# Giving the state matmuls of an attention kernel PSUM banks of their own, and packing three kinds of small matmuls into common runs

## The chip, the cores and the metric

The kernel runs on one core of a Trainium2 chip. The metric is the time of one execution on the device in microseconds (us), as a median over several executions; lower is better. The "span" in a profile is the same execution from its first to its last instruction, some 1.8 us shorter than the time.

## The reference

A block-wise linear attention with a decaying state feeds a feed-forward layer with a sine in it:

```python
for b in range(nb):                       # blocks of 64 positions, 12 of them
    intra = einsum('bhic,bhjc->bhij', qb, kb) * Dmask      # scores, masked
    intra = einsum('bhij,bhjd->bhid', intra, vb)
    inter = einsum('bhid,bhde->bhie', qb * lam_pow, kv_state)
    out[:, :, sl] = intra + inter
    kv_state = lam_block * kv_state + einsum('bhsd,bhse->bhde', kb * rev_pow, vb)
...
h = x @ w_in                              # x: 3072 tokens of 512 = the attention output
s = sin(alpha * h)
g = h + s * s / (alpha + 1e-09)
out = g @ w_out
```

## The kernel before

Tokens go through in six groups of 512. Each group has four attention *units* (24 in all), then 16 first-layer feed-forward blocks and 16 second-layer blocks of four 128x128 by 128x512 matmuls each. The order of all work on all engines is written out by hand in one list. An item names what is done, for which unit or block, on which engine (T TensorE, A ScalarE, V VectorE, G GpSimd, S SyncE, which issues the loads), and for PSUM users in which bank. Each engine follows its own items in that order.

Three item kinds use 64x64 quarters of the array: `s` (scores, 16 matmuls), `k` (state matmuls, 8 or 16) and `o` (masked scores times values, 16). The other TensorE items use the whole array: `oi` (query times state), `f1`, `f1a` and `f2` (feed-forward; `f1a` is half a block), `tq` and `tk` (transposes), `w` (warm-up matmuls on zeros), `lt` (the two halves of the last output tile); a single small `ap` belongs to the start. I call neighbouring `s`, `k` and `o` items with no whole-array item between them a *run*.

The parts that the change touches:

```python
BANK = ("h0", "h1", "h2", "h3", "s0", "s1")       # + "okv", one tile over two banks
HOLD = (0, 14)            # loads of group 1 wait for this first-layer block
...
def kvmm(u, bank, **_):                           # item k
    if u < 8:
        kps[u] = [psum([P, P], FP32, "kvp", i)[:] for i in bank]
    else:                                         # spare columns of the output pair
        okv[u] = ps.tile([P, 2, 512], FP32, name="okv", tag="okv", bufs=1)
        kps[u] = [okv[u][:, c, 2 * P:3 * P] for c in range(2)]
    ...
def interm(u, **_):                               # item oi
    okv[u] = ps.tile([P, 2, 512], FP32, name="okv", tag="okv", bufs=1)
    ...
def outev(u, c, eng, **_):                        # item x: output pair to SBUF
    cs = slice(c, c + 1) if u in XSPLIT else slice(0, 2)      # XSPLIT = (1, 2, 3)
    copy(eng, xt[g][:, 2 * hh:2 * hh + 2, bb, cs, :]..., okv[u][:, cs, 0:2 * P]...)
```

`kc` copies a state out of PSUM, `a` adds and decays it, `m` masks scores, `sin`, `sqr` and `stt` are the sine, its square and the sum of the feed-forward part, `ld` loads q, k or v of a unit, `tdq` and `tdk` transpose it by DMA, `wi` and `wo` load weights.

Of the kernel before, what the change touches and what calls it, by code (L numbers as in the profile page):

```python
# [18 lines left out]
tab:V ld.0.0:S sq.0:V ld.0.1:S sk.0:G w.4:T:h2 tq.0:T:2 tk.0:T:5 ld.0.2:S cv.0:A ld.1.0:S ld.1.1:S  # L19
k.0:T:0,1 a.0.0:V sk.1:V ld.1.2:S tcq.0:A tck.0:A w.4:T:s0 s.0:T kc.0.0:A sq.1:G oi.0:T tq.1:T:0  # L20
tcq.1:A tk.1:T:2 tck.1:A ld.2.0:S ld.2.1:S m.0.0:V m.0.1:V kc.0.1:V sq.2:V cv.1:A o.0:T x.0.0:A
sk.2:V s.1:T tq.2:T:0 tcq.2:A tk.2:T:2 tck.2:A w.3:T:h1 k.1:T:1,0 kc.1.0:A ld.2.2:S ld.3.0:S
ld.3.1:S ld.3.2:S wi.0:G wi.1:G sq.3:G cv.2:G cv.3:G n.0.0:G wi.2:G wi.3:G wo.0:G kc.1.1:A m.1.0:V
m.1.1:V a.1.0:V sk.3:V s.2:T wo.1:G a.0.1:G n.0.1:G m.2.0:V m.2.1:V oi.1:T tq.3:T:1 tcq.3:A tk.3:T:2
k.2:T:0,3 o.1:T x.1.0:V a.2.0:V tck.3:A w.3:T:s0 s.3:T kc.2.0:A kc.2.1:A x.1.1:A w.3:T:okv oi.2:T
o.2:T x.2.0:A m.3.0:V m.3.1:V x.2.1:A k.3:T:1,2 kc.3.0:A kc.3.1:A a.3.0:V ap:T al:V f1a.0.0:T:0
f1a.0.1:T:3 oi.3:T o.3:T f1a.0.2:T:4 f1a.0.3:T:5 x.3.0:V x.3.1:A f1.0.0:T f1.0.1:T sin.0.0:A
sin.0.1:A sqr.0.0:V sqr.0.1:G n.2.0:G wo.2:G f1.0.2:T f1.0.3:T sin.0.2:A stt.0.0:V sin.0.3:A
sqr.0.2:A sqr.0.3:A stt.0.1:V stt.0.2:V stt.0.3:V f1.0.4:T:2 sin.0.4:A sqr.0.4:V a.2.1:G n.2.1:G
f1.0.5:T:1 f1.0.6:T:0 sin.0.5:A sin.0.6:A sqr.0.5:V sqr.0.6:G stt.0.4:V stt.0.5:V stt.0.6:V  # L30
f1.0.7:T:3 f1.0.8:T:5 f1.0.9:T:4 sin.0.7:A sqr.0.7:A sin.0.8:A sin.0.9:A sqr.0.8:G sqr.0.9:G wo.3:G
n.3.0:G a.3.1:G stt.0.7:V stt.0.8:V f1.0.10:T:2 w.2:T:h0 f1.0.11:T:0 n.1.0:G stt.0.9:V sin.0.10:A
sqr.0.10:A stt.0.10:V a.1.1:G f2.0.0.0:T:3 sin.0.11:A sqr.0.11:V f1.0.12:T:5 f1.0.13:T:4 sin.0.12:A
sqr.0.12:A sin.0.13:A stt.0.11:V f1.0.14:T:2 sin.0.14:A sqr.0.13:A stt.0.12:V f2.0.0.1:T
f2.0.1.0:T:1 f1.0.15:T:0 sin.0.15:A f2.0.1.1:T f2.0.1.2:T sqr.0.14:G sqr.0.15:G f2.0.0.2:T
stt.0.13:V stt.0.14:V stt.0.15:V f2.0.2.0:T:2 f2.0.0.3:T oc.0.0:A f2.0.2.1:T f2.0.1.3:T ld.4.0:S
ld.4.1:S ld.4.2:S sq.4:G sk.4:G cv.4:A tq.4:T:3 tk.4:T:5 tcq.4:V tck.4:V oc.0.1:V ld.5.0:S ld.5.1:S
f2.0.2.2:T s.4:T m.4.0:V k.4:T:0,3 f2.0.2.3:T a.4.0:V m.4.1:V ld.5.2:S ld.6.0:S kc.4.0:A kc.4.1:A
cv.5:A ld.6.1:S ld.6.2:S ld.7.0:S ld.7.1:S ld.7.2:S oc.0.2:A sq.5:G sk.5:G tq.5:T:4 tk.5:T:1 oi.4:T
sq.6:G k.5:T:0,3 o.4:T sk.6:G cv.6:G sq.7:G tcq.5:A tck.5:V kc.5.0:A kc.5.1:V a.5.0:V n.5.0:G sk.7:G  # L40
s.5:T m.5.0:V x.4.0:A ld.8.0:S tq.6:T:2 tk.6:T:1 tck.6:A ld.8.1:S ld.8.2:S ld.9.0:S ld.9.1:S
f2.0.3.0:T:3 tcq.6:A m.5.1:V oi.5:T k.6:T:0,1 o.5:T a.6.0:V s.6:T kc.6.0:A ld.9.2:S ld.10.0:S
ld.10.1:S ld.10.2:S kc.6.1:A x.5.0:A tq.7:T:2 tcq.7:A f2.0.3.1:T tk.7:T:0 m.6.0:V m.6.1:V tck.7:V
oi.6:T f1a.1.0:T:1 o.6:T cv.7:G k.7:T:2,0 kc.7.0:A cv.8:A x.6.0:A n.1.1:G a.7.0:V s.7:T m.7.0:V
f2.0.3.2:T f2.0.3.3:T m.7.1:V oi.7:T o.7:T n.6.0:G n.4.0:G kc.7.1:V f1a.1.1:T:5 f1a.1.2:T:0 a.6.1:G
sq.8:G f1a.1.3:T:2 sk.8:G sq.9:G oc.0.3:A x.7.0:A f1.1.0:T f1.1.1:T f1.1.2:T f1.1.3:T f1.1.4:T:3
sin.1.0:A sin.1.1:A sqr.1.0:V sqr.1.1:V sk.9:G stt.1.0:V sin.1.2:A sqr.1.2:G sin.1.3:A sin.1.4:A
f1.1.5:T:4 f1.1.6:T:1 stt.1.1:V sqr.1.3:A stt.1.2:V sin.1.5:A stt.1.3:V sq.10:G k.8:T sqr.1.4:G
sin.1.6:A sqr.1.5:A sqr.1.6:A f1.1.7:T:0 kc.8:V ld.11.0:S f1.1.8:T:5 stt.1.4:V stt.1.5:V stt.1.6:V
sin.1.7:A cv.9:G k.9:T sin.1.8:A kc.9:V sk.10:G sqr.1.7:A sqr.1.8:A stt.1.7:V stt.1.8:V cv.10:G  # L50
sq.11:G n.3.1:G tdq.8:S tdq.9:S tdk.8:S f1.1.9:T:2 f1.1.10:T:3 f1.1.11:T:1 k.10:T sin.1.9:A
ld.11.1:S sk.11:G sqr.1.9:A ld.11.2:S tdk.9:S ld.12.0:S kc.10:A sin.1.10:A s.8:T sqr.1.10:A
f1.1.12:T:0 m.8.0:V a.8.0:G a.9.0:G m.8.1:V oi.8:T sq.12:G tdq.10:S tdk.10:S ld.12.1:S a.4.1:G s.9:T
o.8:T tdq.11:S tdk.11:S ld.12.2:S stt.1.9:V ld.13.0:S st.0.2.0:S f1.1.13:T:2 sin.1.11:A cv.11:A
stt.1.10:V sqr.1.11:A a.10.0:G x.8.0:A m.9.0:V m.9.1:V f2.1.0.0:T:3 n.10.0:G stt.1.11:V n.8.0:G
a.8.1:G ld.13.1:S st.0.1.0:S st.0.0.0:S st.0.0.1:S ld.13.2:S ld.14.0:S ld.14.1:S oi.9:T ld.14.2:S
tdq.12:S sin.1.12:A o.9:T x.9.0:V sin.1.13:A s.10:T m.10.0:V f2.1.0.1:T k.11:T f1.1.14:T:1 m.10.1:V
kc.11:V s.11:T oi.10:T a.11.0:G st.0.2.1:S m.11.0:V m.11.1:V ld.15.0:S ld.15.1:S ld.15.2:S ld.16.0:S
ld.16.1:S cv.12:A o.10:T x.10.0:A sqr.1.12:A f2.1.0.2:T sqr.1.13:G sin.1.14:A oi.11:T stt.1.12:V
o.11:T x.11.0:A stt.1.13:V f1.1.15:T:5 sqr.1.14:G sin.1.15:A sqr.1.15:A f1.2.0:T:4 f1.2.1:T:0  # L60
sin.2.0:A stt.1.14:V sqr.2.0:A sin.2.1:A sqr.2.1:A stt.1.15:V stt.2.0:V stt.2.1:V f1.2.2:T:2
sin.2.2:A sqr.2.2:A stt.2.2:V n.4.1:G st.0.1.1:S sk.12:G n.6.1:G f2.1.0.3:T k.12:T n.11.0:G a.5.1:G
sq.13:G tdq.13:S sq.14:G n.5.1:G f1.2.3:T:4 f1.2.4:T:1 sin.2.3:A sqr.2.3:A f1.2.5:T:0 sin.2.4:A
sin.2.5:A n.8.1:G tdk.12:S ld.16.2:S cv.13:A st.0.3.0:S kc.12:V f2.1.1.0:T:2 f2.1.1.1:T sqr.2.4:A
cv.14:A stt.2.3:V f1.2.6:T:4 f2.1.1.2:T f2.1.1.3:T sqr.2.5:A n.9.0:G a.12.0:G stt.2.4:V stt.2.5:V
sk.13:G sin.2.6:A tdk.13:S k.13:T f1.2.7:T:1 kc.13:V oc.1.0:A f1.2.8:T:0 sqr.2.6:A sin.2.7:A
sqr.2.7:A oc.1.1:V f2.1.2.0:T:3 stt.2.6:V sk.14:G n.12.0:G s.12:T m.12.0:V sk.15:G sq.15:G k.14:T
kc.14:A m.12.1:V tdq.14:S sin.2.8:A stt.2.7:V f2.1.2.1:T f2.1.2.2:T oi.12:T a.13.0:G n.7.0:G s.13:T
o.12:T m.13.0:V a.7.1:G n.7.1:G x.12.0:A m.13.1:V cv.15:G a.9.1:G n.9.1:G st.0.3.1:S f2.1.2.3:T
f1.2.9:T:1 tdq.15:S tdk.14:S oc.1.2:A oi.13:T o.13:T x.13.0:V f1.2.10:T:3 sk.16:G s.14:T ld.17.0:S  # L70
ld.17.1:S tdk.15:S st.1.0.0:S k.15:T m.14.0:V f2.1.3.0:T:2 f2.1.3.1:T sqr.2.8:G stt.2.8:V a.14.0:G
sin.2.9:A sqr.2.9:G sin.2.10:A sqr.2.10:A kc.15:A cv.16:G m.14.1:V n.13.0:G sq.16:G a.15.0:G sq.17:G
stt.2.9:V oi.14:T f1.2.11:T:0 sin.2.11:A sqr.2.11:A s.15:T o.14:T st.1.0.1:S st.1.2.0:S ld.17.2:S
ld.18.0:S stt.2.10:V m.15.0:V x.14.0:A f1.2.12:T:1 f2.1.3.2:T f1.2.13:T:3 stt.2.11:V sin.2.12:A
sqr.2.12:A sin.2.13:A m.15.1:V stt.2.12:V a.10.1:G sqr.2.13:G stt.2.13:V oi.15:T o.15:T f1.2.14:T:0
x.15.0:A sin.2.14:A f1.2.15:T:1 sin.2.15:A sqr.2.14:A sqr.2.15:G f1.3.0:T:4 f1.3.1:T:3 f1.3.2:T:5
sin.3.0:A sin.3.1:A sqr.3.0:A f2.1.3.3:T stt.2.14:V stt.2.15:V f1.3.3:T:0 sqr.3.1:A stt.3.0:V k.16:T
sin.3.2:A stt.3.1:V f1.3.4:T:4 oc.1.3:V sqr.3.2:A sin.3.3:A sqr.3.3:A stt.3.2:V stt.3.3:V sin.3.4:A
sqr.3.4:A stt.3.4:V kc.16:A f1.3.5:T:3 f1.3.6:T:2 f2.2.0.0:T:1 f2.2.0.1:T cv.17:A f1.3.7:T:4
f1.3.8:T:5 f2.2.0.2:T sin.3.5:A sqr.3.5:A stt.3.5:V sin.3.6:A sin.3.7:A sin.3.8:A sqr.3.6:A  # L80
sqr.3.7:A ld.18.1:S ld.18.2:S ld.19.0:S ld.19.1:S ld.19.2:S cv.18:G sk.17:G sk.18:G ld.20.0:S
tdq.16:S ld.20.1:S sq.18:G sk.19:G stt.3.6:V stt.3.7:V cv.19:G n.10.1:G sq.19:G sqr.3.8:A tdq.17:S
a.11.1:G n.11.1:G n.14.0:G a.14.1:G n.14.1:G f1.3.9:T:0 f2.2.0.3:T f1.3.10:T:2 f1.3.11:T:3 stt.3.8:V
sin.3.9:A tdq.18:S tdk.16:S s.16:T sqr.3.9:A a.16.0:G oc.2.0:A ld.20.2:S ld.21.0:S ld.21.1:S k.17:T
tdk.17:S sin.3.10:A kc.17:A sqr.3.10:G sin.3.11:A st.1.3.0:S st.1.1.0:S stt.3.9:V f2.2.1.0:T:1
oi.16:T m.16.0:V m.16.1:V f2.2.1.1:T sq.20:G s.17:T o.16:T stt.3.10:V sqr.3.11:A f2.2.1.2:T n.15.0:G
sk.20:G f2.2.1.3:T m.17.0:V tdk.18:S x.16.0:V m.17.1:V st.1.3.1:S stt.3.11:V k.18:T kc.18:V
f1.3.12:T:2 s.18:T a.17.0:G a.18.0:G st.1.1.1:S sk.21:G cv.20:G sin.3.12:A k.19:T ld.21.2:S kc.19:A
f1.3.13:T:3 sin.3.13:A f2.2.2.0:T:0 oi.17:T st.2.0.0:S a.19.0:G tdq.19:S tdq.20:S st.2.0.1:S
# [37 lines left out]
def kernel(  # L127
# [24 lines left out]
    RING = 8  # L152
    GATE = (2, 1)
    HOLD = (0, 14)
    XSPLIT = (1, 2, 3)
    N0 = 28
    assert NDC == HP

# [474 lines left out]
```

## Time and profile before

The median was 219.93 us (219.68 to 220.19 in 3 runs).

| what | before |
|---|---|
| runs of `s`, `k`, `o` in the order list | 46, of which 33 in units 8 to 23 |
| first matmul of group 0's first `f1` item, of group 1's | 21.42 us, 56.89 us |
| start of the last output tile | 210.58 us |
| last weight block (`wo.3`) requested, landed | 31.56 us, 39.02 us |

The `f1` items in question only finish what `f1a` items began; I call their first matmul the group's *first whole feed-forward matmul* all the same. The start times are read off TensorE's instructions in the trace. The copies of the output pair are two rows in the view of groups (line, engine, operation, tiles, shape, count, then busy us in total and mean ns of one, then what the engine waited for in front of them):

```profile
L279 ACT CAST xt<-okv 128x512 bf16<-128x512 f32 x16 | 9.4, 589 | 7.9 <-PE okv L466 7.9
L281 DVE CAST xt<-okv 128x512 bf16<-128x512 f32 x5 | 3.4, 689 | 4.7 <-PE okv L466 4.7
```

Nearly all are whole copies, and they wait only for the `o` matmuls, not for each other.

### The profile page before, as it was taken

What the parts mean: (1) busy time and instruction counts of PE and PEld (TensorE: products, weight loads), DVE (VectorE), ACT (ScalarE), POOL (GpSimd) and SP (SyncE); (2) the same over time, 40 slices, a digit from 0 to 9 for tenths busy, and PEclk for the clock granted to TensorE, in tenths of its full rate; (3) what the DMA queues carried; (4) which work ended last, traced back from release to release, by engine and by line L of the source; (5) the groups of instructions that cost most, each with busy time, mean ns of one, the idle gap of its engine ahead of it and who ended that gap; (6) DMA issues with size and microseconds to landing.
All of it is one profiled execution on the core that took longest, in us unless ns stands there. A gap on an engine that the chain in (4) does not pass through costs nothing.

```text
span 218.1 us, 5357 instructions
## 1 busy us (share of the span) xinstructions
PE 207.9 (95%) x2096; PEld 107.8 (49%) x2096; DVE 125.1 (57%) x212; ACT 128.8 (59%) x238; POOL 139.6 (64%) x207
## 2 busy tenths in 40 slices
PE   8688999989999999999999999999999999999992
PEld 6456544456744544454444545444455444444462
DVE  3794786186499775659574737565575225454110
ACT  3663976256699499646899644596545337580011
POOL 5478677699599999999598689568731325330000
PEclk9999999999999999999999999999999999999999
DMA  5999999999977799969998969352512210412244
GB/s 136 299 235 166 206 198 186 278 300 282 212 198 121 225 233 290 170 120 248 270 141 209 200 148 214 82 120 48 120 27 51 48 26 0 91 33 48 58 92 92
DMA packets 63849, 33.92 MB, mean 155 GB/s; under 512 B 19648, under 2 KB 60880, under 8 KB 63824
## 3 DMA queue, kind: packets, MB, share of 16 engines
q1 hardware_dynamic: 59488, 29.31, 58.7%
q0 software_dynamic: 4224, 4.19, 12.5%
q8 instruction: 16, 0.26, 0.6%
q10 hardware_dynamic: 112, 0.07, 0.1%
q14 instruction: 9, 0.07, 0.1%
HBM read 27.28 MB, written 6.29 MB: 154 GB/s over the span
## 4 chain that ended last, share of the span: by engine, by line
PE 78%; POOL 6%; DVE 4%; SPq 3%; issue 3%; DMA 2%; ACT 2%; POOLq 0%; ACTq 0%
PE ops L532 36%; PE hps L489 31%; SPq L256 3%; PE sp L365 3%; DMA st_k<-in_k_dram 2%; PE okv L466 2%; PE okv L452 2%; PE ops L555 2%; POOL KD L297 2%; DVE gall L523 1%; PE okv L401 1%; POOL QL L297 1%; POOL s L518 1%; POOL VB L281 1%; DVE ST L375 1%
## 5 line engine op out<-in xcount | busy, mean ns | idle before, releaser
L523 DVE SCALAR_TENSOR_TENSOR gall<-s,r_sb,hps 128x512 bf16<-128x512 bf16 x96 | 69.1, 744 | 37.8 <-POOL s L518 18.8
L489 PE MATMUL hps<-xt,w_in_sb 128*128 128x512 bf16 (+1 forms) x416 | 90.5, 363 | 0.1
L532 PE MATMUL ops<-w_out_sb,gall 128*128 128x512 bf16 x368 | 86.9, 379 | 0.0
L509 ACT ACTIVATE s<-hps,alpha_sb 128x512 bf16<-128x512 f32 x96 | 63.6, 687 | 30.5 <-PE hps L489 27.5
L518 POOL TENSOR_TENSOR s<-s 128x512 bf16<-128x512 bf16 x34 | 35.2, 1043 | 41.6 <-ACT s L509 38.9
L489 PEld LDWEIGHTS <-w_in_sb 128*128 128x128 bf16 x416 | 38.8, 98 | 38.4 <-issue 0.2
L532 PEld LDWEIGHTS <-gall 128*128 128x128 bf16 x368 | 34.5, 98 | 39.6
L375 DVE TENSOR_TENSOR ST<-sp,mask 128x512 bf16<-128x512 f32 x48 | 31.3, 685 | 7.6 <-PE sp L365 7.3
L516 ACT ACTIVATE s<-s 128x512 bf16<-128x512 bf16 x56 | 34.6, 633 | 1.4 <-DVE gall L523 0.5
L297 POOL TENSOR_TENSOR QL<-st_q,E 128x512 bf16<-128x512 f32 x22 | 22.9, 1044 | 2.8 <-DMA st_q<-in_q_dram 2.3
L279 ACT COPY ob<-ops 128x512 f32<-128x512 f32 (+1 forms) x15 | 8.4, 557 | 26.7 <-PE ops L532 24.1
L297 POOL TENSOR_TENSOR KD<-st_k,R 128x512 bf16<-128x512 f32 x21 | 21.8, 1044 | 0.6 <-DVE tab L281 0.6
L431 POOL TENSOR_TENSOR kvbd<-kvx,LBD 128x256 bf16<-128x256 f32 x32 | 19.7, 616 | 2.5
L279 ACT CAST xt<-okv 128x512 bf16<-128x512 f32 (+1 forms) x20 | 10.8, 547 | 10.7 <-PE okv L466 9.2
L427 POOL TENSOR_TENSOR kvx<-kva,kvs 128x128 f32<-128x128 f32 x32 | 14.6, 457 | 3.8 <-DVE kva L281 2.9
L281 DVE COPY ob<-ops 128x512 f32<-128x512 f32 x10 | 6.9, 689 | 13.6 <-PE ops L532 13.6
L365 PE MATMUL sp<-QT 64*64 64x128 bf16 x384 | 10.0, 220 | 0.6 <-ACT QT L279 0.4
L466 PE MATMUL okv<-ST,VB 64*64 64x128 bf16 x384 | 10.0, 219 | 0.6 <-DVE ST L375 0.6
L439 POOL TENSOR_TENSOR kvs<-kvx,LHP 128x128 f32<-128x128 f32 x24 | 9.6, 409 | 0.0
L365 PEld LDWEIGHTS <-QT 64*64 64x64 bf16 x384 | 6.6, 106 | 5.6 <-issue 3.5
L452 PE MATMUL okv<-QT,kvbd 128*128 128x128 bf16 x80 | 8.6, 220 | 0.7 <-DVE kvbd L431 0.3
L452 PEld LDWEIGHTS <-kvbd 128*128 128x128 bf16 x80 | 6.0, 98 | 5.8 <-DVE kvbd L431 0.9
(60 smaller groups left out, 114.5 us busy)
## 6 DMA issues: line engine op xcount, KB each, us to landing
st_q<-in_q_dram SPq DMA_DIRECT2D x24, 256.0 KB, 5.1
st_k<-in_k_dram SPq DMA_DIRECT2D x24, 256.0 KB, 5.3
st_v<-in_v_dram SPq DMA_DIRECT2D x24, 256.0 KB, 4.9
out_dram<-ob SPq DMA_DIRECT2D x46, 128.0 KB, 2.4
w_in_sb<-in_moe_w_in_dram POOLq DMA_DIRECT2D x4, 512.0 KB, 7.8
w_out_sb<-in_moe_w_out_dram POOLq DMA_DIRECT2D x4, 512.0 KB, 11.2
QT<-QL SPq DMA_TRANSPOSE x16, 3.5
QT<-KD SPq DMA_TRANSPOSE x16, 3.0
```

The source lines that it names most:

```text
L279: nc.scalar.copy(out=out, in_=in_)
L297: eng.tensor_tensor(out=t[:], in0=stage[u, j][:].rearrange("p h two e -> p two h e"), in1=tab[:, :, hh * HH:(hh + 1) * HH].unsqueeze(3).to ...
L365: nc.tensor.matmul(out=sp[hd][half[c], par, hp, :], lhsT=QT[half[hd], 1, par, hp, half[c]], rhs=QT[half[hd], 0, :, hp, half[c]], start=Tru ...
L375: nc.vector.tensor_tensor(out=stm[u][:, hd], in0=sps[u][hd][:], in1=mask[:].unsqueeze(2).to_broadcast([P, 2, 2, P]), op=ALU.mult)
L431: eng.tensor_tensor(out=kvbd[u, c][:], in0=x.unsqueeze(2).to_broadcast([P, 2, 2, D]), in1=LBD[:, 2 * hh:2 * hh + 2, :].unsqueeze(3).to_bro ...
L452: nc.tensor.matmul(out=okv[u][:, c, hp * P:(hp + 1) * P], lhsT=sts[c][:, hp].rearrange("p two e -> p (two e)"), rhs=QT[:, 0, :, hp, half[c ...
L489: f1mm[g, f] = nc.tensor.matmul(out=hps[g, f][:].rearrange("p (b i) -> p b i", b=2)[:, bs] .rearrange("p b i -> p (b i)"), lhsT=w_in_sb[:, ...
L509: nc.scalar.activation(out=s1[g, f][:], in_=hps[g, f][:], func=ACTF.Sin, scale=alpha_sb[:, f:f + 1])
L516: nc.scalar.activation(out=s2[g, f][:], in_=x[:], func=ACTF.Square)
L518: eng.tensor_tensor(out=s2[g, f][:], in0=x[:], in1=x[:], op=ALU.mult)
L523: nc.vector.scalar_tensor_tensor(out=gall[g][:, f, :], in0=s2.pop((g, f))[:], scalar=r_sb[:, f:f + 1], in1=hps.pop((g, f))[:], op0=ALU.mul ...
L532: nc.tensor.matmul(out=ops[g, m][:], lhsT=gall[g][:, f, m * P:(m + 1) * P], rhs=w_out_sb[:, f, :], start=(f == 0), stop=(f == NFC - 1))
```

## The change

The intent: the tile `okv` over two banks held both the outputs and, for units from 8 on, the states, so a state group could not stand right behind the preceding unit's outputs. The output pair becomes two tiles in banks 6 and 7, each copied by itself, a state group gets any banks that are free (22 of the 24 out of the other six; units 4 and 13 still use the output banks), and the order list is written anew so that `o`, `k` and `s` items of different units stand together.

```diff
-    HOLD = (0, 14)
+    HOLD = (0, 12)
...
-    BANK = ("h0", "h1", "h2", "h3", "s0", "s1")
+    BANK = ("h0", "h1", "h2", "h3", "s0", "s1", "oa", "ob")
...
-        if u < 8:
-            kps[u] = [psum([P, P], FP32, "kvp", i)[:] for i in bank]
-        else:
-            okv[u] = ps.tile([P, 2, 512], FP32, name="okv", tag="okv", bufs=1)
-            kps[u] = [okv[u][:, c, 2 * P:3 * P] for c in range(2)]
+        kps[u] = [psum([P, P], FP32, "kvp", i)[:] for i in bank]
...
-        okv[u] = ps.tile([P, 2, 512], FP32, name="okv", tag="okv", bufs=1)
+        okv[u] = [psum([P, 512], FP32, "okv", i) for i in (6, 7)]
...
-        cs = slice(c, c + 1) if u in XSPLIT else slice(0, 2)
-        copy(eng, xt[g][:, 2 * hh:2 * hh + 2, bb, cs, :].rearrange("p hp c i -> p c hp i"),
-             okv[u][:, cs, 0:2 * P].rearrange("p c (hp i) -> p c hp i", hp=2))
+        copy(eng, xt[g][:, 2 * hh:2 * hh + 2, bb, c, :],
+             okv[u][c][:, 0:2 * P].rearrange("p (hp i) -> p hp i", hp=2))
... (the whole order list is new; one stretch of TensorE's items in it:)
-... s.9:T o.8:T f1.1.13:T:2 f2.1.0.0:T:3 oi.9:T o.9:T s.10:T f2.1.0.1:T k.11:T f1.1.14:T:1 s.11:T ...
+... s.9:T o.8:T k.10:T:0,1 f2.1.0.3:T oi.9:T o.9:T s.10:T k.11:T:2,0 f2.1.1.0:T:1 oi.10:T k.12:T:2,0 s.11:T o.10:T ...
```

## The prediction

> **What bounds the kernel now.** The work is 24 attention units, four to each of six token groups, and per token group a feed-forward part of 16 first-layer blocks (four full-array matmuls each) and 16 second-layer blocks (four each). I read the page first: engines, then the slices.
>
> ```profile
> span 218.1 us, 5357 instructions
> PE 207.9 (95%) x2096; PEld 107.8 (49%) x2096; DVE 125.1 (57%) x212; ACT 128.8 (59%) x238; POOL 139.6 (64%) x207
> ...
> DMA  5999999999977799969998969352512210412244
> ```
>
> TensorE (PE) is busy for 95% of the span, and no other engine passes 64%. The DMA engines are full from the second slice to the eleventh (5.5 to 60 us). So only two things can shorten this kernel: less TensorE time, or an earlier start of the dense part. The second view, windows cut at the first full feed-forward matmul (21.4 us), at the first transposes of token group 1 (43.0), at the first full one of group 1 (56.9) and at TensorE's end (214.3), says how much idle time there is:
>
> ```profile
> 21.40:43.00 21.60, 21.35 (x109) 10.44 (x108) 13.22 (x20) 14.21 (x25) 15.05 (x21) 1.00 1.13 215
> 43.00:56.90 13.90, 13.01 (x273) 8.65 (x272) 9.18 (x19) 7.41 (x18) 13.35 (x18) 1.00 1.10 286
> 56.90:214.30 157.40, 157.07 (x1426) 76.81 (x1423) 89.06 (x136) 96.10 (x168) 97.02 (x140) 1.00 0.60 131
> ```
>
> First the length, then TensorE's busy time: idle are 0.25, 0.89 and 0.33 us. Waits of TensorE after 21.4 us thus sum to 1.5 us; a change there must shorten TensorE's own work. The granted clock is 1.00 throughout. Before 21.4 us there is real idle time, and TensorE's 47 warm-up matmuls (7.7 us busy) hide more.
>
> The third view, the chain that ended last, shows what one group of small matmuls costs (start, length, what; 88 to 96 us):
>
> ```profile
> 88.17 0.25 PE okv L401 x16
> 88.42 1.83 PE hps L489 x8
> 90.25 0.86 PE ops L532 x4
> 91.11 0.35 PE sp L365 x16
> 91.58 1.83 PE ops L532 x8
> 93.42 0.22 PE okv L452 x4
> 93.64 0.35 PE sp L365 x16
> 93.99 0.22 PE okv L466 x16
> 94.21 0.97 PE ops L532 x4
> 95.18 0.86 PE hps L489 x4
> ```
>
> Groups s (L365), k (L401) and o (L466) use 64x64 quarters of the array; everything else uses all of it. Group s takes 0.35 us after full-array work, while o right behind it, with as many matmuls of the same width, takes 0.22: entering the quarter mode costs 0.13. Four full matmuls take 0.86, but 0.97 behind a quarter group: leaving costs 0.11. One run of quarter groups, however many it holds, pays **0.24 us**. The k at 91.46 (between 91.11+0.35 and 91.58) took 0.12 behind an s, against 0.25 alone at 88.17: different kinds share a run freely.
>
> **What the skill says.** "TensorEngine Tiling (Array Packing)", Key Properties: changing the tiling mode, not just the tile, drains TensorE. The trace agrees: that is the 0.13 and 0.11. "PSUM — Partial Sum Buffer", PSUM bank collisions raise a hardware error: two engines must not use one bank's quadrant at once. That is why a state matmul (k) put into spare columns of the output pair must wait for that pair's copies, and why k could seldom stand directly behind the preceding unit's o. The trace agrees only in so far as 23 of 46 runs hold one group. "VectorE: DVE Perf Modes", The TRN2 errata: ScalarE and VectorE pay a fixed cost per instruction. The trace agrees: ScalarE's 128x512 copy xt<-okv is 589 ns, its 128x256 copy 378, so two halves cost 167 ns more than one whole.
>
> **The change, part by part.**
>
> *Fewer mode changes.* I counted the runs of s, k and o uninterrupted by a full-array item in the two order lists. Before 46, after 33. The start (units 0 to 3) has 8 in both and is not dense. For units 4 to 7 it goes from 5 to 6; for the rest from 33 to 19. So 13 fewer runs x 0.24 = **-3.1 us**, nearly all in the stretch from 56.9 us, where TensorE has 0.33 us of idle time. This lies wholly on the path. No matmul of the product is removed.
>
> *More copies, off the path.* The output pair becomes two tiles, copied separately: 48 half copies for 27 (16 whole and 4 half on ScalarE, 5 and 2 on VectorE). ScalarE: 29 x 0.378 = 11.0 us for 10.8. VectorE: 19 x 0.42 = 8.0 for 4.2. State copies: 40 for 32, near 1.1 and 0.1 us more. Squares move: ScalarE 56 to 51 (-3.2), VectorE 6 to 10 (+2.0), GpSimd 34 to 35. All stay below 66% of the span: **0** on the path, except where a copy ends a wait.
>
> *The start.* Here the chain is DMA, VectorE, ScalarE, TensorE:
>
> ```profile
> 14.03 0.69 DVE KD L297
> 14.71 1.02 DVE ST L375 x2
> ...
> 18.64 0.65 ACT xt L279 x2
> 19.29 0.18 ACT kva L279
> 19.47 0.02 issue
> 19.49 0.44 DVE kvbd L431
> 19.93 0.05 issue
> 19.98 0.28 PE okv L452 x2
> 20.26 0.35 PE okv L466 x16
> 20.61 4.46 PE hps L489 x32
> ```
>
> The last attention group of unit 3 runs at 20.26 because its decayed state waits for a ScalarE state copy queued behind output copies. The new order gives that state copy to VectorE, before unit 3's masks, and starts masking unit 2 without the key scaling of unit 3 ahead of it (that goes to GpSimd). Adding row durations along the new VectorE queue: unit 1's masks end near 13.3 (13.22 before), two state copies (0.57) and a decay (0.42) give 14.1, unit 2's masks (1.28) 15.4, then unit 3's key (landed at 14.0 as now, scaled on GpSimd behind the query, 15.4), transpose and copy 16.3, scores 16.8 to 17.2, masks 18.5, last o 18.9. Two half blocks (0.86) follow: first full feed-forward matmul near 19.8, against 21.42. The first weight block landed at 17.9 and the second at 20.4, needed at 18.7 and 21.5: they don't bind. **-1.6 us**, if the queues mesh as added.
>
> *Group 0's feed-forward, up to 43 us.* The old order has a three-fold pause near 29.5 us (0.19 idle, a two-matmul warm-up, restart: 0.35 + 0.43 = 0.8 us between 29.22, where the blocks would end, and 30.00). With eight banks instead of six, the new order runs fifteen first-layer blocks ahead. Per block VectorE needs 0.68 (4 in a row took 2.71) and for 7 of 16 a square of 0.51, so 0.91 on the mean, TensorE 0.86: VectorE falls behind by 0.05 a block, some 0.7 us over fifteen, which the two further banks cover. **-0.8 us.**
>
> *Group 1's attention, 43 to 57 us.* TensorE had 0.89 us of waits there, on full DMA and GpSimd (13.35 busy of 13.90). The new order starts the loads after first-layer block 12 instead of 14 but has one second-layer block fewer to hide in, one mode run more, one warm-up more (2 x 0.11). I put **+0.7 us**.
>
> *The rest.* State matmuls now take banks from the feed-forward blocks, and fewer blocks separate scores from their output matmuls. The old order waits 0.33 us from 56.9 us on; a newly packed one may wait about 0.8 more. **+0.8 us**, a judgement.
>
> *The end.* TensorE's last matmul to the end is 218.1 - 214.3 = 3.8 us in both.
>
> Sum: -3.1 - 1.6 - 0.8 + 0.7 + 0.8 = -4.0 in span. The sum of worked parts without my two allowances is -5.5. I take -4.6, between them and nearer the sum, because the allowances are the softer half: 219.93 - 4.6 = 215.3 us.
>
> **The rivals.**
>
> *Waits take the place of drains.* Packing o, k and s of neighbouring units brings each scores group nearer its masks: a unit needs two masks of 0.69 us, while only one or two blocks of 0.86 stand between. For it: GpSimd, which makes states and scales, is 87% busy from 56 to 110 us (47.18 of 54). Against: VectorE is at 57%, and the old order had only 0.6 us of TensorE waits on masks. It would give back 2 to 3 us: 217.5 to 218.5.
>
> *The loads bind the start and group 1.* DMA is full to 60 us, so earlier requests need not land earlier; in the trace unit 7's last load landed at 49.4 us, only 7.5 before group 1's first full block. For it: slices full of nines. Against: the eight weight blocks landed between 2.5 and 4.0 us apart, so some slack exists. Then only the mode changes remain: 219.9 - 3.1 = 216.8.
>
> *Everything meshes.* Start, pause and mode changes all pay, with no new waits: 219.9 - 5.5 = 214.4, or 213 if the loads come 2 us sooner.
>
> *Half copies block.* If ScalarE and VectorE delay sines, banks come free late. 6 us more work over both at 60% speaks against it; perhaps 1 us.
>
> **Range and chances.** The mode changes are well measured (-2.7 to -3.4). The start and group 0 are an addition over queues (-0.5 to -3), and waits are open (0 to +3). Eight in ten: 213.0 to 217.8. Faster by over 2% means below 215.5, just above my number: 0.54. Same 0.45. Slower 0.01, as nothing removed was hidden work.
>
> **What would show it.** Mode runs: s, k or o groups at 0.35 or 0.25 us in front and 0.97 behind should number 33, and TensorE busy plus idle from group 1's first full block to its end should fall from 157.4 by about 3.4 less new waits. The first full block should stand near 19.8 us, group 1's near 54. Idle time of TensorE beyond 1.5 us in the dense part, before masks, states or copies, would show the first rival. I am wrong if a run of three groups pays per group, if the start doesn't move, or if TensorE waits over 3 us after 57 us.

## The result, and the profile after

The changed kernel took 216.81 us in the median (216.46 to 217.79 in 4 runs), the kernel before 219.81 us beside it. The ratio is 0.987, with a 95% interval of 0.983 to 0.991. The change is thus 3.0 us or 1.3% faster, which counts as "the same" at a threshold of 2%. The time is inside the predicted range and 1.5 us above the predicted point. The profiled execution was the fastest of the four (216.46 us), so the traces differ by 3.4 us in span where the medians differ by 3.0.

The page of the kernel after begins so:

```profile
span 214.7 us, 5454 instructions
...
PE 206.3 (96%) x2116; PEld 109.7 (51%) x2116; DVE 129.6 (60%) x234; ACT 123.8 (58%) x244; POOL 141.5 (66%) x208
```

TensorE's busy time fell by 1.6 us (207.9 to 206.3), although it has 20 matmuls more, all of them warm-up. No other engine came near the bound. Windows of the kernel after, cut at the same events as the prediction's windows of the kernel before (now at 20.22, 42.57, 55.80 and 210.9 us; length, then TensorE's busy time, then the other engines, the clock, the DMA share and GB/s):

```profile
20.22:42.57 22.35, 21.77 (x110) 10.58 (x109) 14.45 (x24) 12.56 (x21) 15.53 (x22) 1.00 1.19 236
42.57:55.80 13.23, 12.10 (x283) 8.21 (x282) 8.73 (x19) 9.02 (x24) 11.70 (x16) 1.00 1.15 257
55.80:210.90 155.10, 154.10 (x1414) 77.36 (x1411) 92.35 (x150) 92.16 (x176) 99.63 (x142) 1.00 0.64 133
```

Length minus busy is TensorE's idle time: 0.58, 1.13 and 1.00 us, together 2.7 us where it was 1.5. So the change shortened TensorE's work and gave part of it back as waits. The events place the gain. The windows don't hold quite the same work (after, one more second-layer block of 0.865 us stands before the first transposes of group 1; half a first-layer block of 0.44 us less and a state group of 0.12 more stand before group 1's first whole matmul), so I correct for it:

| stretch | before | after | gained, for equal work | of it in this stretch |
|---|---|---|---|---|
| to group 0's first whole matmul | 21.42 | 20.22 | 1.20 | 1.20 |
| to the first transposes of group 1 | 42.95 | 42.57 | 0.38 + 0.865 = 1.24 | 0.04 |
| to group 1's first whole matmul | 56.89 | 55.80 | 1.09 - 0.44 + 0.12 = 0.77 | -0.47 |
| to the start of the last output tile | 210.58 | 207.12 | 3.46 | 2.69 |

The last row is where the quarter-array groups were packed. The chain that ended last in the kernel after shows a run of three kinds there (start, length, what):

```profile
72.14 0.35 PE sp L367 x16
72.48 0.22 PE okv L459 x16
72.71 0.12 PE kvp L399 x16
72.83 0.97 PE ops L524 x4
```

This is a scores group, another unit's output group and a third unit's state group. Only the first is long (0.35 against 0.22), and the block behind them takes 0.97 against 0.86: one entry and one exit, 0.24 us, for all three.

Two waits show where gains went. The first is in the same view at 32 to 43 us:

```profile
32.11 8.70 DMA w_out_sb<-in_moe_w_out_dram
...
40.85 1.89 PE ops L524 x8
```

The last weight block, requested by GpSimd at 32.11 us, landed at 40.81, and TensorE stood still 0.58 us for it. Before, it landed at 39.02 and TensorE came to it only at 40.36. After, it is requested 0.55 us later and takes 8.70 us instead of 7.46, and the loads for group 1 start at 29.94 us instead of 34.51, ahead of that request. That these loads made it slower is likely, but no run separates the two.

The second stands at 115.85 us, in front of unit 17's scores (`sp`):

```profile
110.20 5.61 DMA QT<-KD
...
115.85 0.42 PE sp L367 x16
```

TensorE waited 0.87 us for the DMA transpose of a scaled key. From its issue to its landing that transpose took 5.61 us. SyncE issues the loads of q, k and v, the DMA transposes and all output stores but one, one after the other, and its queue had hardly a gap around that time (start, length, what it issued):

```profile
108.14 0.62 SPq L258 DMA_DIRECT2D st_q<-in_q_dram  x1
108.87 1.23 SPq L344 DMA_TRANSPOSE QT<-QL  x1
110.20 1.25 SPq L344 DMA_TRANSPOSE QT<-KD  x1
111.54 2.72 SPq L344 DMA_TRANSPOSE QT<-QL  x1
```

Here a load holds the queue for 0.6 us, a transpose for 1.2 us and more. So that key's transpose could hardly have been issued earlier without moving something else.

The output copies, which were whole:

```profile
L281 ACT CAST xt<-okv 128x256 bf16<-128x256 f32 x29 | 9.8, 374 | 12.6 <-PE okv L459 12.4
L283 DVE CAST xt<-okv 128x256 bf16<-128x256 f32 x19 | 7.7, 419 | 11.0 <-PE okv L459 11.0
```

Twice as many, all of half size, still waiting for the `o` matmuls alone.

### The profile page after: what moved, and what is told of

Same layout as the page of the kernel before. It is cut to its first block, busy times and chain, and to the rows that moved or that the text cites. A ratio compares the mean times of both kernels' runs of the same rounds, so it can differ in the third digit from the quotient of the medians.

```text
span 214.7 us, 5454 instructions
## 1 busy us (share of the span) xinstructions
PE 206.3 (96%) x2116; PEld 109.7 (51%) x2116; DVE 129.6 (60%) x234; ACT 123.8 (58%) x244; POOL 141.5 (66%) x208
## 4 chain that ended last, share of the span: by engine, by line
PE 72%; DMA 11%; POOL 4%; SPq 4%; ACT 4%; issue 2%; DVE 1%; POOLq 0%; ACTq 0%
PE ops L524 31%; PE hps L481 30%; DMA w_out_sb<-in_moe_w_out_dram 4%; SPq L258 4%; DMA st_v<-in_v_dram 3%; DMA QT<-KD 3%; PE sp L367 2%; PE okv L459 2%; ACT s L501 2%; DMA st_k<-in_k_dram 2%; PE ops L547 2%; PE okv L445 2%; POOL KD L299 1%; PE kvp L399 1%; POOL QL L299 1%
## 5 line engine op out<-in xcount | busy, mean ns | idle before, releaser
L481 PE MATMUL hps<-xt,w_in_sb 128*128 128x512 bf16 (+1 forms) x416 | 87.5, 363 | 0.0
L510 POOL TENSOR_TENSOR s<-s 128x512 bf16<-128x512 bf16 x35 | 36.4, 1048 | 37.8 <-ACT s L501 37.1
L508 ACT ACTIVATE s<-s 128x512 bf16<-128x512 bf16 x51 | 31.6, 633 | 1.0 <-DVE gall L515 0.4
L283 DVE COPY ob<-ops 128x512 f32<-128x512 f32 x12 | 8.3, 690 | 26.7 <-PE ops L524 23.4
L281 ACT COPY ob<-ops 128x512 f32<-128x512 f32 (+1 forms) x13 | 7.2, 555 | 23.3 <-PE ops L547 12.9
L281 ACT CAST xt<-okv 128x256 bf16<-128x256 f32 x29 | 9.8, 374 | 12.6 <-PE okv L459 12.4
L283 DVE CAST xt<-okv 128x256 bf16<-128x256 f32 x19 | 7.7, 419 | 11.0 <-PE okv L459 11.0
L281 ACT COPY kva<-kvp 128x128 f32<-128x128 f32 x26 | 6.4, 273 | 9.2 <-PE kvp L399 8.2
L281 ACT COPY QT<-pt 128x512 bf16<-128x512 bf16 x9 | 5.2, 585 | 10.1 <-PE pt L326 10.1
L281 ACT CAST VB<-st_v 128x512 bf16<-128x512 f32 x14 | 8.6, 622 | 1.6 <-DMA st_v<-in_v_dram 1.6
```

Source lines behind the costliest of these rows:

```text
L281: nc.scalar.copy(out=out, in_=in_)
L283: eng.tensor_copy(out=out, in_=in_)
L481: f1mm[g, f] = nc.tensor.matmul(out=hps[g, f][:].rearrange("p (b i) -> p b i", b=2)[:, bs] .rearrange("p b i -> p (b i)"), lhsT=w_in_sb[:, ...
L508: nc.scalar.activation(out=s2[g, f][:], in_=x[:], func=ACTF.Square)
L510: eng.tensor_tensor(out=s2[g, f][:], in0=x[:], in1=x[:], op=ALU.mult)
```

## The experiments

The theory: packing saves 0.24 us for each run that it does away with; the banks and the half copies earn nothing by themselves but make the packing possible; and the gains at the start and in group 0 don't reach the end, because TensorE then arrives earlier at something that a transfer sets (the last weight block, the DMA transposes). The rivals: a run's cost grows with the number of its groups, or the drains are cheaper than read off, so that the packing paid less; or the new order waits for masks, states and copies. All outputs are right. Medians are given with the range of the runs; the kernel before took 219.86, 219.91 and 219.67 us in the three batches. A new-order kernel varies by 1 to 3 us from run to run, the kernel before by 0.5 to 1, so differences between new-order kernels below about 1 us are not settled by their times. Each run has one profile, so what is said of its waits holds for that one execution.

### a_base: the changed kernel once more

No edit. It is the yardstick of the other runs.

> The changed kernel again, on the chip of the runs beside it, as their baseline. Both theories: 216.5 to 217.3 us, 0.985 to 0.989 of the kernel before. The question beside it is whether the two TensorE waits of the first profile (0.58 us for the last second-layer weight block at 40.9 us, 1.13 us before a state group at 52.5 us without a releaser) stand at the same places.

Measured: 216.78 us (215.62 to 217.95), ratio 0.986 (0.983 to 0.989). In its profile TensorE waits 0.30 us for the last weight block, 0.93 us at 105.0 us for unit 16's transpose and 0.87 us at 116.5 us for unit 17's. The result and the two kinds of wait repeat; the exact places vary: the wait at 52.5 us shrank from 1.13 to 0.31 us, those at 92.7 us (0.35, for a bank) and 105.0 us are new.

### split_all: put the mode changes back

From unit 9 on, single whole-array matmuls of the block that follows a run are moved between the run's groups. No work is added and all buffers stay; there are 28 more mode changes of in-and-out.

```diff
... (TensorE's items alone)
-s.9:T o.8:T k.10:T:0,1 f2.1.0.3:T
+s.9:T p2.1.0.3.0.1:T o.8:T p2.1.0.3.1.2:T k.10:T:0,1 p2.1.0.3.2.4:T
... (p2.g.m.j.a.b and p1.g.f.a.b: matmuls a to b-1 of the block; 28 such breaks)
```

> The changed kernel with each run of quarter-array groups of units 8 to 23 broken up again, by single full-array matmuls taken from the block that follows the run: 28 more mode changes, no instruction more, same buffers and banks. Theory 1 (each run costs 0.24 us of mode change): +28 x 0.24 = +6.7 us over the changed kernel, 223.5 us. Rival (the gain came from free banks, fewer waits or the start, and a run costs little): within 1 us of the changed kernel.

Measured: 221.32 us (220.80 to 222.60), ratio 1.008 (1.006 to 1.010): 4.5 us over a_base, where 28 x 0.24 is 6.7. The chain of this run shows what a break costs:

```profile
121.65 0.32 PE ops L547
121.97 0.24 PE kvp L405 x8
122.21 0.32 PE ops L547
122.53 0.24 PE kvp L405 x8
```

The single whole-array matmul (`ops`) takes 0.32 us instead of 0.216, the state group 0.24 instead of 0.12. From unit 17's scores to unit 23's, the distance to a_base grew from 0.70 to 4.47 us over 14 breaks, 0.27 us each. From unit 9's to unit 17's it grew from -0.12 to 0.70 us only, for the other 14. There a_base has its two transpose waits of 0.93 and 0.87 us and the one of 0.35 at 92.7 us, and split_all has none of them: being later, it found the transposes landed. These 2.15 us are most of the 2.5 us that are missing from 14 x 0.24; the rest isn't placed. So the drains cost what was read off, and the rival "cheaper drains" falls.

### wo3early: request the last weight block earlier

```diff
-wo.2:G x.3.1:V
+wo.2:G wo.3:G x.3.1:V
... (and wo.3:G taken away from its later place)
```

> The changed kernel with the request of the last second-layer weight block moved up on GpSimd to right behind the one before (about 20 us instead of 32 us). Theory 1 (that block's landing at 40.8 us made TensorE wait and the wait reaches the end): the wait of 0.58 us goes and the time falls by 0.6 to 0.7 us. Rival (unit 4 to 7's loads are pushed back by as much, and bound group 1's start): the wait goes, but the first full feed-forward matmul of group 1 stays near 55.8 us and the time within 0.2 us.

Measured: 215.77 us (215.64 to 216.81), ratio 0.983 (0.981 to 0.984). The wait for the weights is gone from the profile, and the first transposes of group 1 start at 41.75 us (42.31 in a_base). But this lead doesn't reach the end: one wait of 0.74 us at 75.2 us for unit 11's transpose has come, and unit 11's scores start 0.28 us later than a_base's. The profile ends 1.1 us ahead all the same (the last unit's scores at 158.08 against 159.22), because the waits at 105.0 and 116.5 us are gone; that the early request removed those isn't shown. The median is 1.0 us below a_base's, but the intervals of the ratios overlap.

### startlate: give the start's gain back

Ten more warm-up matmuls stand in front of unit 3's outputs, so that the dense part starts later by what was gained.

```diff
-w.6:T:h1 oi.3:T
+w.16:T:h1 oi.3:T
```

> The changed kernel with ten more warm-up matmuls right before unit 3's output, so that the first full feed-forward matmul starts 1.1 us later. Theory 1 (the earlier start ran into the wait for the last weight block at 40.8 us, which is fixed by the DMA queues): the wait shrinks from 0.7 us to nothing and the time rises by only 0.4 us. Rival (a later start reaches the end in full): +1.1 us.

Measured: 216.29 us (215.56 to 218.69), ratio 0.986 (0.982 to 0.989). The first whole matmul is at 21.62 us, 1.37 us later than in a_base, yet the time is not longer. In the traces the distance to a_base is 1.46 us at unit 4's scores, 1.4 at unit 11's, 1.0 at unit 13's, 0.74 at unit 16's, and -0.20 from unit 17's to the end. I had thought that the weight block in group 0 would swallow it. It didn't: that wait is still there (0.40 us at 42.06), because the request and the loads moved along. The delay was swallowed between 75 and 117 us, most of it at unit 17, where a_base waits 0.87 us and this run not at all. Its wait for unit 16 remains:

```profile
105.74 0.42 PE L367 MATMUL sp<-QT 64*64 64x128 bf16 x16 [0.93 <-DMA QT<-KD]
```

So a start 1.4 us earlier is worth nothing that these runs can resolve (about 1 us) at the end of this kernel.

### spfix: issue the transposes earlier

SyncE issues the transposes of units 16 and 17 ahead of loads that stood in front of them.

```diff
-ld.18.0:S ... tdq.16:S tdk.16:S
+tdq.16:S tdk.16:S ... ld.18.0:S
-ld.20.1:S ... ld.20.2:S ... tdq.17:S tdk.17:S
+tdq.17:S ... tdk.17:S ld.20.1:S ... ld.20.2:S
```

> The changed kernel with two pairs of DMA transposes moved up in the SyncE queue: those of unit 16 ahead of unit 18's three loads, those of unit 17 ahead of two loads of unit 20, one of 21 and a store. In the last profile of the changed kernel scores 16 and 17 waited 0.93 and 0.87 us for these. Theory (these two waits give back what start and mode changes gained, and pin the time at 105 and 116 us): both waits go, the time falls by 1.3 to 1.8 us and spreads less. Rival (the transposes are late for a full DMA, whatever the order of issue): waits remain, time within 0.4 us.

Measured: 217.27 us (216.66 to 219.32), ratio 0.989 (0.985 to 0.992). It isn't faster. The profiled execution, a slower one of 218.29 us, waits 1.46 us for the weights, and no longer before the scores of units 16 and 17 but 1.58 us at 106.6 us, before unit 15's product with its state. The wait moved.

### combo: both repairs

```diff
... (the edits of wo3early and of spfix)
```

> Both moves together: the last second-layer weight block requested early, and the transposes of units 16 and 17 moved up. Theory (the waits stand one behind the other on TensorE, and the later pair no longer hides what the earlier move gains): 2.0 to 2.6 us under the changed kernel, 214.2 to 214.8 us. Rival (each hides the other): no better than the better of the two, 215.4 us or more.

Measured: 216.81 us (215.87 to 217.99), ratio 0.986 (0.983 to 0.989), a miss. The chain of this run names the new wait:

```profile
99.39 2.41 issue
...
101.83 1.04 POOL QL L300
...
103.92 0.62 POOL kvbd L425
...
104.59 0.34 PE okv L446 x3
```

GpSimd stands 2.41 us ahead of scaling unit 18's query, whose load landed at 101.76 us because spfix put it behind the transposes. In GpSimd's order unit 15's decayed state (`kvbd`) comes after that, and TensorE waited 1.96 us for it. An engine that follows its items in order hands a late load on to a unit that never needed it.

### combo_late: both repairs and a later start

```diff
... (combo, and w.6 -> w.16)
```

> The run before with ten more warm-up matmuls before unit 3's output, which start the dense part 1.1 to 1.4 us later. With the waits of the changed kernel in place such a delay did not reach the end (216.3 against 216.8 us). Theory (it had been absorbed by the waits for transposes of units 16 and 17): now +0.9 to +1.4 us over combo. Rival (something else absorbs it): within 0.4 us of combo.

Measured: 217.20 us (216.26 to 218.35), ratio 0.988 (0.985 to 0.990): 0.4 us over combo for ten more warm-up matmuls, where I had expected 0.9 to 1.4. Here too most of the later start is swallowed, though the waits for the transposes of units 16 and 17 are gone: they aren't the only place that absorbs it. The profiled execution waits 0.98 us at 76.2 us for a transpose and 1.36 us at 106.6.

### bufonly: the free banks without the new order

The old order list with the two output tiles and half copies; states of units from 8 on get banks among the first six (unit 15's both output banks and unit 11's one of them, for want of a free one), with the smallest disturbance that I found in the list.

```diff
-k.8:T ... kc.8:V            (old order list)
+k.8:T:5,2 ... kc.8.0:V kc.8.1:V
... (so for all units from 8 on; x.u.0 and x.u.1 for each x.u.0)
```

> The buffers of the change alone: two output tiles copied by halves, state matmuls of units 8 to 23 in banks of their own (two of the sixteen, for want of a free bank, stay wholly or in half in the output banks), but in the order of the kernel before, with its 46 runs. Theory (the gain is the saved mode changes, the banks only allow the order): 219.5 to 220.5 us, as before. Rival (free banks and shorter waits for copies are the gain): 217 to 218 us.

Measured: 227.61 us (226.16 to 227.97), ratio 1.034 (1.032 to 1.036), far slower than I expected. TensorE waits in front of state groups among others, the longest in this line of the timeline:

```profile
85.49 0.31 PE L400 MATMUL kvp<-VB,KD 64*64 64x64 bf16 x14 [2.39 <-DVE gall L516]
```

The state group waits for VectorE to finish a feed-forward block (`gall`) in the bank that it was given. In an order written for six rotating banks, a state takes one out of the rotation. The run shows only that these banks in an order not written for them are no gain; as my choice of banks made the loss, what the best choice would give in the old order stays untested.

### halves: the half copies alone

As bufonly, but the states stay in the output banks as before (`k.8:T:6,7` and so on), so only the two tiles and the half copies are new.

```diff
-okv[u] = ps.tile([P, 2, 512], FP32, name="okv", tag="okv", bufs=1)
+okv[u] = [psum([P, 512], FP32, "okv", i) for i in (6, 7)]
... (and one copy for each half, in the old order list)
```

> The order of the kernel before, its 46 runs and its state matmuls in the output pair's banks, but the pair as two tiles with half copies (48 for 27) and the states copied by halves. Theory (more copies lie off TensorE's path): within 0.7 us of the kernel before, 219.2 to 220.6 us. Rival (they delay sines and copies, and cost what the banks gain): 1 us or more above it. The run bufonly, which gave the states banks out of the six that the feed-forward blocks rotate through, cost 7.7 us; this one shows how much of that was the halves.

Measured: 219.10 us (218.78 to 219.87), ratio 0.997 (0.996 to 0.999). The half copies cost nothing; if anything they save 0.6 us.

### kshared: the new order without the free banks

In the new order, 13 more of the 16 state groups of units 8 to 23 go into the output banks, as before the change (unit 13's is there already; those of units 8 and 9 stay apart). As they must then wait for the output copies, they are put last in their run, and the copies in front of them.

```diff
-s.9:T o.8:T k.10:T:0,1 ... x.8.0:A x.8.1:A ... kc.10.0:A
+s.9:T o.8:T x.8.0:A x.8.1:A k.10:T:6,7 ... kc.10.0:A
```

> The new order, but thirteen of the sixteen state groups of units 8 to 23 put into the two output banks, each behind the copies of the output before it; the state group stands last in its run where it must. Wrong in nothing but time. Theory (the new order needs free banks: a state right behind an output would wait for its two half copies, 0.4 to 0.75 us each): TensorE waits appear before state groups, +4 to +8 us over the changed kernel. Rival (free banks don't matter, only the order): within 1 us of it.

Measured: 223.95 us (223.50 to 224.50), ratio 1.019 (1.017 to 1.021). That is 4.3 us slower than the kernel before, where a_base was 3.1 us faster than it in its own batch: 7.4 us lost. The waits in front of state groups for output copies are 2.4 us in all behind VectorE (6 times) and 2.4 us behind ScalarE (5 times), such as

```profile
119.13 0.31 PE L400 MATMUL kvp<-VB,KD 64*64 64x64 bf16 x8 [0.51 <-DVE xt L284]
```

and feed-forward blocks waited another 1.4 us. So the packed order needs the banks. It is the closest test that stays free of races; it also moves copies and state groups, so the 7.4 us are not the banks' worth to the last tenth.

### wo3sq: the earlier weight block, and GpSimd's scaling of unit 18's query later

To spare GpSimd the wait that combo showed, the item that scales that query moves to just ahead of the same unit's key.

```diff
... (wo3early, and:)
-sq.18:G cv.15:A ... sk.18:G
+cv.15:A ... sq.18:G sk.18:G
```

> The early request of the last weight block (215.8 us when run before) and, on GpSimd, the query scaling of unit 18 moved from before unit 15's state to behind unit 17's key scaling, so that a late load of unit 18 no longer holds up unit 15's state or unit 17's key. Theory (GpSimd's order with loads in it is what pins the time between 95 and 117 us): the waits there shrink, 214.8 to 215.8 us. Rival (full DMA queues pin it): 215.8 to 217.

Measured: 216.13 us (214.99 to 217.41), ratio 0.985 (0.982 to 0.988). Its profiled execution has the shortest span of all (213.2 us), but the median is no better than wo3early's (a miss: 214.8 to 215.8 was expected), and 0.99 us before unit 16's scores remain.

### combo3: all three repairs

```diff
... (wo3sq, and the edit of spfix)
```

> The same, with the transposes of units 16 and 17 moved up as in spfix and combo. There the wait moved to unit 15's state (1.96 us at 104.6 us in combo), because unit 18's query load, now issued later, held up GpSimd's queue ahead of that state; here that scaling comes later. Theory (as for wo3sq): that wait goes and so do those for the transposes; 214.3 to 215.3 us. Rival: 216 us or more, the wait showing up a third time elsewhere.

Measured: 216.83 us (214.99 to 218.13), ratio 0.987 (0.983 to 0.990), a miss again. A wait of 1.68 us now stands at 114.7 us, before a first-layer block: the third place. The repairs show that between 95 and 117 us loads, transposes and GpSimd's order hold each other; which of them is the limit (SyncE's issue time, the DMA engines, GpSimd) stays open.

The fastest version is wo3early, 1.7% below the kernel before and 0.3% below the changed kernel by ratio, which these runs don't tell apart from no difference.

## Why the prediction was right or wrong

**Its range held; its point was 1.5 us too low, and "faster by over 2%", to which it gave 0.54, did not come.** The main mechanism is the one predicted; that several terms agree in size with this one profile is partly luck, as a_base's profile of the same kernel shows.

**Mode changes: right.** From group 1's first whole matmul on, 14 runs fewer should save 14 x 0.24 = 3.4 us; with the 0.8 us allowed for new waits, 2.6. The trace shows 2.69, with 0.67 us more of idle time than before: together again 3.36. The saving repeats, the waits set against it don't: in a_base's profile, with its 2.15 us of waits, the same stretch gained only 1.0. The three-kind run at 72.14 us pays once, and split_all measures 0.27 us for a run's break where nothing else waits. The listed 3.1 us was the net of 13 runs; the run that units 4 to 7 have more was counted in it and again in group 1's allowance. Without that slip the sum would have been -4.2 or -4.3 rather than -4.0.

**Copies: right.** They were predicted to cost nothing, and halves shows it. On ScalarE and VectorE the halves took 9.8 and 7.7 us, no more than the 11.0 and 8.0 worked out.

**The start: right mechanism, 0.4 us too large, and of little use.** The first whole matmul came 1.20 us sooner, not 1.6. The queues meshed as added up to unit 3's masks (worked out to end at 18.5 us, in the trace at 18.57). The failed step is "last o 18.9. Two half blocks (0.86) follow": the new order has two of the four half blocks in front of that `o`, TensorE was in them until 19.07 us, and the `o` ended at 19.42. What I hadn't asked at all is whether the gain reaches the end. startlate answers that: most of it is lost in waits up to 117 us. The range was wide enough for it, the working was not.

**Group 0's feed-forward: the step that failed.** The pause near 29.5 us did go, as worked out: from 20.22 to 31.48 us the first-layer matmuls run unbroken. But the -0.8 us silently assumes that no other wait follows, and I had checked the landings of the first two weight blocks only. The last one landed 1.3 us earlier than needed in the old order; in the new one, which requests group 1's loads 4.6 us sooner, it landed at 40.81, where TensorE would have come to it near 40.1. TensorE stood 0.58 us and paid about 0.15 for the restart, 0.73 in all, and the stretch gained 0.04 us. wo3early takes the wait away, and in its profile the stretch gains 0.79 us for equal work: the predicted 0.8, so it was this wait alone that the step had missed.

**Group 1's attention: right in size by luck.** Predicted +0.7, measured +0.47. In the one profile of the changed kernel this contains 1.13 us in front of unit 7's state group at 52.5 us, for which the profile names no releaser; in spfix it was 0.95, in a_base 0.31, in wo3early 0.24, in startlate 0. Its cause stays open. Without it the stretch needed no allowance: for equal work it is 0.34 us shorter than before in a_base's profile.

**Shading the sum: wrong.** The worked sum was -4.0, and I took -4.6 because I held the allowances for the softer half. It was the gains at the start and in group 0 that were soft: they had been worked out along one engine's queue each, without asking what else comes due. The measured terms, -1.20 - 0.04 + 0.47 - 2.69, sum to -3.46, within 0.1 of the span's difference.

**The rivals.** "Waits take the place of drains" came true in small: idle time in the dense part grew from 1.5 to 2.7 us. But it was not masks that TensorE waited for: 1.45 us were waits for transfers, and the 1.13 us at 52.5 us have no named releaser. (Its 217.5 to 218.5 should have read 217.3 to 218.3, 2 to 3 us above 215.3.) "The loads bind the start and group 1" named 216.8 us, and that was the median, by coincidence: the start did move, so the loads didn't bind there, and the waits that took the gain back stand elsewhere.

## What to carry to other kernels

Count the changes of array mode, not the small groups: here 0.24 us for each run, however many groups stand in it, and free banks pay by allowing the packing (no run shows a gain from them alone). When an engine is dense in front of a stretch that is fed by transfers, a saving ahead of that stretch is worth only what the transfers leave of it; before crediting it, delay the start on purpose and see whether the end moves. When a new order asks for some loads sooner, look up the landing of every transfer that shares the engines with them, the last one too.

## What the Trainium skill lacked or had wrong

- "TensorEngine Tiling (Array Packing)", Key Properties, says that a change of tiling mode drains TensorE, and gives no cost. In the traces it is 0.13 us into the quarter mode and 0.11 us out of it, 0.24 us for a run; 14 breaks put in on purpose cost 0.27 us each.
- "TensorE: Matmul & The Clock Gate", Back-to-back issue gap, gives 131 ns as the sustained spacing of weight-load and matmul pairs of 512 columns, and calls the isolated gap of 216 ns an overcount there. Here each matmul of the feed-forward blocks has its own weight load, and four take 0.86 us, 216 ns each: the measurement sides with the isolated figure.
- "Perfetto Trace Analysis", Matmul Optimizations, advises to use all eight PSUM banks. Both kernels use all eight; what decided was which work shares a bank with which. The same order took 216.78 us with nearly all states apart from the outputs and 223.95 us with 13 more state groups in the output banks.
- "DMA: Bandwidth & Descriptors", DMA Transpose (X-bar), lists constraints, and no time for which a transpose holds the queue of the engine that issues it; the page's only such times stand in its table on trn3, in a column for "previous generations" that doesn't name this chip. Here it is 1.2 us and up to 2.7 us on SyncE for a 128x512 tile in bf16, beside 0.6 us for most loads of 256 KB.
